# Block sums of values from the chunks already loaded, instead of a second load

## The chip, the cores and the metric

The kernel runs on one core of a Trainium2 chip. The time is the device time of one execution in microseconds; all times below are microseconds unless marked ns. A core has five engines that run side by side and wait for each other through semaphores: TensorE (PE: matmuls, with its weight loads shown as PEld), VectorE (DVE), ScalarE (ACT), GpSimd (POOL) and SyncE (SP). Transfers are issued from queues; here GpSimd issues the loads that convert float32 to bfloat16, and SyncE issues crossbar transposes (DMA_TRANSPOSE: 16-bit data turned on the way from SBUF to SBUF) and a part of the output stores. All of them are carried out by the same 16 transfer engines.

## What is computed

For 4 batches of 8 heads, 768 tokens and head dimension 64, a sparse attention followed by a gated feed-forward block:

```python
k_sum = k.reshape(B, H, nb, block, D).max(axis=3)          # block = 32, nb = 24
v_sum = v.reshape(B, H, nb, block, D).mean(axis=3)
scores_l = scale * q @ k.T          where |i - j| < 16, else -1e9
scores_s = scale * q @ k_sum.T + log(block)
a = softmax(concat(scores_l, scores_s))
x = a @ concat(v, v_sum)            # then 3072 tokens x 512
g, val = x @ w_gate, x @ w_val      # 512 -> 1536
out = x + sigmoid(x @ w_res) * ((gelu(g) * val) @ w_out)
```

So each query looks at its 31 nearest keys and at 24 block summaries: the maximum of the keys of a block and the mean of its values. The change concerns the mean of the values.

## The kernel before

**Units.** The work goes in 8 units of 384 tokens, two for each batch; unit u computes the feed-forward block of half u % 2 of batch u // 2, and in its second part the attention of unit u + 1. A unit has 12 steps `fo`: `fo_step` runs four matmuls for g (w_gate) and four for vv (w_val, L398), ScalarE makes the gelu `ge` (L404), VectorE multiplies it with vv to `gvT` (L405). After the steps follow, interleaved, the scores of the next unit (`s_step`, L330), their exponent (L336, L339) and mask (L347), the attention output (`av_step`, L362, with the normalization L370 and L372 that gives `xn`), the gate matmuls (`res_step`, L416), the output matmuls `f` (`ffn_step`, L432) and `end_step` (L437, L439, and the store of 256 KB, L443). The attention output must be turned into `xT` before the next unit's first matmuls. For units 0 to 2 this is done wholly by TensorE (`xt_step`, transposes `xp` in L381, copied by ScalarE); from unit 3 on three of the four head pairs are turned by crossbar on SyncE's queue (`xt_dma`, L386) and one by TensorE. From unit 3 on a unit opens with twelve matmuls `gv` (L544) in which the third head pair is used last.

**Data of a batch.** Keys and queries come as rows `k_sb`, `q_sb` (`load_rows`, L175, 16 loads of 96 KB from GpSimd's queue). For batches 2 and 3 they are turned by crossbar, three transposes a head pair (`turn_batch`, L251 and L254), into the window layout `kW` and into `qT`; `k_rest` then makes on VectorE the block maxima and the neighbor columns, five operations a head pair (L209 to L215). Values come as chunks of 128 tokens straight into the window layout `vext` (`load_values`, L100, seven loads), where each even window tile is a whole chunk of 128 consecutive tokens, shifted by 16. `v_spread` (L291, L294) copies them into the odd tiles, and `vsum_bc` (L300, L303) writes the block means into rows 96 to 127 of every tile.

**Block means of values.** Batch 0 and 1 get them by matmuls (`vsum_sum`). For batches 2 and 3 the values are loaded a second time as rows `v_sb` (eight more loads in `load_rows`), turned by crossbar (`turn_values`, four transposes, L261), summed by VectorE in four reductions (`block_sums`, L267, at the last four steps of units 2 and 4), turned back (`turn_sums`, L271, in units 3 and 5) and spread with the factor 1/32.

**Order.** The order on every engine is that of the program text; each engine works through its own list and waits where data are missing. A copy on GpSimd of one element of `gvT` (`gate`, L169) holds back the loads behind it until a given step is done. PSUM and SBUF buffers are taken from pools in turn; the pool `mm` of four PSUM banks holds g, vv, gv, r and f.

The places that matter below: batch 2 is loaded in unit 1, behind the gate at step 6, keys, queries and second values first, chunks last; batch 3 is loaded from the end of unit 2 (gate at step 11) and its chunks at the beginning of unit 3. In units 2 and 4 SyncE turns `v_sb` and the first two head pairs at step 0; in units 3 and 5 it turns the sums and the other two head pairs at step 0, and `k_rest` runs at steps 0, 2, 9 and 10. In unit 1 `k_rest` of head pairs 2 and 3 of batch 1 runs at steps 8 and 9.

Of the kernel before, what the change touches and what calls it, by code (L numbers as in the profile page):

```python
# [9 lines left out]
BF16 = mybir.dt.bfloat16  # L10
# [5 lines left out]
def kernel(  # L16
# [11 lines left out]
    nc = tc.nc  # L28
# [43 lines left out]
    warm = const.tile([128, 512], BF16, name="warm")  # L72
    kW = [[const.tile([128, NT, 128], BF16, name=f"kW{i}_{p}") for p in range(NP)] for i in range(2)]
    qT = [[const.tile([128, S], BF16, name=f"qT{i}_{p}") for p in range(NP)] for i in range(2)]
    vext = [const.tile([128, NT, H, D + 1], BF16, name=f"vext{i}") for i in range(2)]
    vsum = [const.tile([128, H, D + 1], BF16, name=f"vsum{i}") for i in range(2)]
    tick = const.tile([1, 1], BF16, name="tick")
    vsT = const.tile([128, NP, 128], BF16, name="vsT")
    vsB = const.tile([128, NP, 128], BF16, name="vsB")
    w_gate = wpool.tile([128, KO, DFF], BF16, name="w_gate")  # L80
    w_val = wpool.tile([128, KO, DFF], BF16, name="w_val")
    w_out = wpool.tile([128, FO, DM], BF16, name="w_out")
# [16 lines left out]
        dst = vext[b % 2][0 if c else WIN:128, 2 * c, :, 0:D] if c < NC else vext[b % 2][64:64 + WIN, NT - 1, :, 0:D]  # L99
        nc.gpsimd.dma_start(out=dst, in_=v[b, :, lo:hi, :].rearrange("h p d -> p h d"))  # L100

    k_sb, q_sb, v_sb, vT = {}, {}, {}, {}

    with tc.manual_schedule():

        def vext_consts(i):
            nc.vector.memset(vext[i][:, :, :, D:D + 1], 1.0)
            nc.vector.memset(vext[i][0:WIN, 0], 0.0)
            nc.vector.memset(vext[i][64:96, NT - 1], 0.0)
            nc.vector.memset(vext[i][64:64 + WIN, NT - 1, :, D:D + 1], 1.0)  # L110
# [58 lines left out]
            nc.gpsimd.tensor_copy(tick[:], t)  # L169

        def load_rows(b):
            for sb, src, name in ((k_sb, k, "k_sb"), (q_sb, q, "q_sb"), (v_sb, v, "v_sb"))[0:2 if b == 1 else 3]:
                sb[b] = (qk1 if sb is v_sb else qk).tile([128, NP, NC, 2 * D], BF16, tag=name, name=name)
                for h in range(H) if b > 1 else (4, 5, 6, 7, 0, 1, 2, 3):
                    nc.gpsimd.dma_start(out=sb[b][:, h // 2, :, h % 2 * D:h % 2 * D + D],  # L175
                                        in_=src[b, h].rearrange("(c p) d -> p c d", c=NC))

        def load_batch(b):
            load_rows(b)
            for c in range(NC + 1):  # L180
                load_values(b, c)

        def turn_pair(src, hp, pool, tag):

# [71 lines left out]
                    in_=q_sb[b][:, hp].rearrange("p c d -> p (c d)"))  # L256

        def turn_values(b):
            vT = qk1.tile([128, NP, S], BF16, tag="k0", name="vT")
            for hp in range(NP):  # L260
                nc.sync.dma_start_transpose(out=vT[:, hp].rearrange("d (c m) -> d c m", c=NC),  # L261
                                            in_=v_sb[b][:, hp].rearrange("p c d -> p (c d)"))
            return vT

        def block_sums(vT, hp):
            with nc.allow_low_precision("block means are bf16 operands"):
                nc.vector.tensor_reduce(out=vsT[:, hp, 96:96 + NB], in_=vT[:, hp].rearrange("d (n w) -> d n w", w=BLK),  # L267
                                        axis=mybir.AxisListType.X, op=ALU.add)

        def turn_sums():  # L270
# [25 lines left out]
        def vsum_bc(b, hp, lo, hi):  # L296
            dst = vext[b % 2][96:128, lo:hi, 2 * hp:2 * hp + 2, 0:D]
            if b < 2:
                src = vsum[b][96:128, 2 * hp:2 * hp + 2, 0:D]
                nc.vector.tensor_copy(dst, src.unsqueeze(1).to_broadcast([32, hi - lo, 2, D]))  # L300
            else:
                src = vsB[96:128, hp].rearrange("p (h d) -> p h d", d=D)
                nc.vector.tensor_scalar_mul(dst, src.unsqueeze(1).to_broadcast([32, hi - lo, 2, D]), 1.0 / BLK)  # L303

        def s_tiles(two=None):
# [145 lines left out]
        def values_step(u, fo):  # L451

            b = u // 2 + 1
            if u in (2, 4) and fo >= FO - NP:
                block_sums(vT[b], fo - FO + NP)
            if u in (3, 5):
                if fo in (1, 3):
                    v_spread(b, 0, HT // 2, fo // 2)
                if 5 <= fo < 9:
                    vsum_bc(b, fo - 5, 0, HT)  # L460
            if u % 2 == 0 and u < NU - 1:
                if fo in (0, 1):
                    v_spread(b - 1, HT // 2, NC, fo)
                if 2 <= fo < 2 + NP:
                    vsum_bc(b - 1, fo - 2, HT, NT)
# [47 lines left out]
            av_part(0, hp, st, *homes[hp], blocks=False)  # L513
        keep_warm(1, wp)
        vsum_sum(0, *MM, (5,), vs, first=False, last=True)
        vsum_out(0, vs, 0, 2, nc.vector.tensor_copy)
        vsum_out(0, vs, 2, 8, nc.scalar.copy)
        for hp in range(NP):
# [3 lines left out]
        firsts = [(w_gate, 0, two[:, 0, :]), (w_val, 0, two[:, 1, :]), (w_gate, 1, None), (w_val, 1, None)]  # L522
        for hp in range(NP):
            xt_step(0, hp, st, *(MM, MM, AO, TT)[hp], nc.scalar.copy)
            if hp:
                firsts = [(w, fo, half_fo(st, w, fo, hp - 1, hp, acc)) for w, fo, acc in firsts]

        for u in range(NU):
# [2 lines left out]
            n = u + 1  # L531
            if u == 1:
                turn_batch(1, 2, NP)
            if u == 3:
                for c in range(NC + 1):
                    load_values(3, c)
            gvT = upool.tile([128, FO, TU], BF16, tag="gvT", name="gvT")
            if u > 2:
                firsts = [(w, fo, ps_mm.tile([128, 512], F32, tag="mm", name="gv"))
# [6 lines left out]
            for fo in range(FO):  # L546
                if u == 0 and fo < 2:
                    for w, _, acc in firsts[2 * fo:2 * fo + 2]:
                        half_fo(st, w, fo, KO - 1, KO, acc)
                    fo_end(gvT, fo, firsts[2 * fo][2], firsts[2 * fo + 1][2])  # L550
                elif u > 2 and fo == 0:
                    fo_end(gvT, fo, firsts[0][2], firsts[1][2])
                elif u > 2 and fo == 1:
                    fo_end(gvT, fo, firsts[2][2], half_fo(st, w_val, fo, 0, KO))
                else:
                    fo_step(st, gvT, fo)
                values_step(u, fo)
                if u == 0 and fo == 4:
                    nc.vector.memset(vsT[:], 0.0)
                    load_rows(1)  # L560
                if u == 0 and fo == 6:
                    vext_consts(1)
                if u == 0 and fo == FO - 1:
                    kw_consts(1)
                    for c in range(NC + 1):
                        load_values(1, c)
                if u == 2 and fo == FO - 1:
                    gate(gvT[0:1, fo, 0:1])
                    load_rows(3)
                if half == 0 and 1 < nb < B and fo == 0:  # L570
                    vT[nb] = turn_values(nb)
                    turn_batch(nb, 0, NP - 2)
                if half == 1 and 1 < nb < B and fo == 0:
                    turn_sums()
                    turn_batch(nb, NP - 2, NP)
                if half == 1 and 1 < nb < B and fo in (0, 2, 9, 10):
                    k_rest(kW[nb % 2][(0, 2, 9, 10).index(fo)])
                if u == 1 and fo == 6:
                    gate(gvT[0:1, fo, 0:1])
                    load_batch(2)  # L580
                if u == 1 and fo in (1, 2, 6, 7):
                    home = TT if fo % 2 else AO
                    if fo < 4:
                        k_step(nb, fo - 1, *home)
                    else:
                        q_step(q_sb[nb], nb, 0, S, fo - 6, *home)
                if u == 1 and fo in (8, 9):
                    k_rest(kW[1][fo - 6])
                if u == 0 and fo >= FO - 4:
                    k_later(kW[0][fo - FO + 4])  # L590
                if u == 0 and fo in (FO - 3, FO - 2):
                    for hp in range(2 * (fo - FO + 3), 2 * (fo - FO + 3) + 2):
                        q_step(qb, 0, TU, S, hp, *(TT if hp % 2 else AO))
# [57 lines left out]
            s_step(n, 3, nst, two=(MM, MM), masked=False)  # L651
            if u < 2:
                mask_part(3, nst)
                xt_step(n, 0, nst, *AO, nc.scalar.copy)
                ffn_step(st, gvT, 1, 6, FO)
                xt_step(n, 1, nst, *TT, nc.scalar.copy)
                res_step(st, 2)
                av_step(n, 2, nst, *AO)
                av_step(n, 3, nst, *TT)
                end_step(u, st, 1)  # L660
                ffn_step(st, gvT, 2, 0, 7)
                xt_step(n, 2, nst, *AO, nc.scalar.copy)
                ffn_step(st, gvT, 2, 7, 10)
            else:
                xt_dma(0, nst)
                xt_dma(1, nst)
                mask_part(3, nst)
                end_step(u, st, 0)
                ffn_step(st, gvT, 1, 0, FO)
                av_step(n, 2, nst, *AO)  # L670
                xt_dma(2, nst)
                av_step(n, 3, nst, *TT)
                res_step(st, 2)
                end_step(u, st, 1)
                ffn_step(st, gvT, 2, 0, 10)
# [34 lines left out]
```

## Time and profile before

| | |
|---|---|
| median of 5 runs | 262.83 (262.47 to 264.88) |
| the profiled execution's own time | 263.37 |
| its span | 261.5 |
| TensorE busy | 251.0 (96%), 2235 matmuls |
| VectorE busy | 177.6 (68%) |
| ScalarE busy | 128.1 (49%) |
| GpSimd busy | 101.2 (39%), nearly all of it issuing loads in the first half |
| transfers issued by GpSimd (queue 0) | 86640 packets, 19.11 MB |
| transfers issued by SyncE (queue 1) | 32480 packets, 10.99 MB |
| read from HBM | 32.51 MB |

Durations are those of one profiled execution, counted from the span's start. The busy time of TensorE is modelled, since matmuls overlap. "Idle before" in brackets is the time an engine stood still before an instruction, with what ended it. A transfer has two times: how long its issue held the queue, and how long it took from issue to landing. The clock row (PEclk) gives the share of TensorE's full clock that was granted in each of 40 slices of the span, in tenths.

### The profile page before, as it was taken

What the parts mean: (1) busy time and instruction counts of PE and PEld (TensorE: products, weight loads), DVE (VectorE), ACT (ScalarE), POOL (GpSimd) and SP (SyncE); (2) the same over time, 40 slices, a digit from 0 to 9 for tenths busy, and PEclk for the clock granted to TensorE, in tenths of its full rate; (3) what the DMA queues carried; (4) which work ended last, traced back from release to release, by engine and by line L of the source; (5) the groups of instructions that cost most, each with busy time, mean ns of one, the idle gap of its engine ahead of it and who ended that gap; (6) DMA issues with size and microseconds to landing.
All of it is one profiled execution on the core that took longest, in us unless ns stands there. A gap on an engine that the chain in (4) does not pass through costs nothing.

```text
span 261.5 us, 5722 instructions
## 1 busy us (share of the span) xinstructions
PE 251.0 (96%) x2235; PEld 139.9 (53%) x2235; DVE 177.6 (68%) x426; ACT 128.1 (49%) x220; POOL 101.2 (39%) x139
## 2 busy tenths in 40 slices
PE   7989999999998999968999999999999999999994
PEld 3545655566544555534555565456545565556544
DVE  4655866594697878757786787588868764674424
ACT  3665369455635637332364435734364536443310
POOL 7996452994789901997370200010000100020000
PEclk9999999999999999997999999999999999999999
DMA  8999999999999999999999695047102200030012
GB/s 154 150 154 196 196 205 195 150 210 129 139 150 157 174 120 148 118 178 203 144 152 80 169 122 90 3 118 160 31 1 74 94 3 0 18 126 27 1 40 80
DMA packets 119146, 30.45 MB, mean 116 GB/s; under 512 B 106064, under 2 KB 116752, under 8 KB 119120
## 3 DMA queue, kind: packets, MB, share of 16 engines
q0 software_dynamic: 86640, 19.11, 85.5%
q1 hardware_dynamic: 32480, 10.99, 25.8%
q8 instruction: 17, 0.28, 0.5%
q14 instruction: 9, 0.07, 0.1%
HBM read 32.51 MB, written 6.29 MB: 148 GB/s over the span
## 4 chain that ended last, share of the span: by engine, by line
PE 83%; DMA 7%; DVE 4%; ACT 2%; POOL 1%; issue 1%; DVEq 0%
PE vv L398 21%; PE g L398 20%; PE f L432 20%; PE r L416 7%; PE gv L544 3%; PE ao L362 3%; DMA k_sb<-in_k_dram 3%; DMA xT<-xn 3%; PE s L330 3%; DMA kf<-in_k_dram 1%; PE xp L381 1%; POOL k_sb L175 1%; DVE th L437 1%; DVE xn L372 1%; DVE o L439 1%; PE tp L226 1%
## 5 line engine op out<-in xcount | busy, mean ns | idle before, releaser
L398 PE MATMUL vv<-xT,w_val 128*128 128x384 bf16 x360 | 74.6, 329 | 0.0
L404 ACT ACTIVATE ge<-g 128x384 f32<-128x384 f32 x85 | 41.8, 491 | 63.6 <-PE g L398 34.9
L398 PE MATMUL g<-xT,w_gate 128*128 128x384 bf16 x340 | 70.5, 329 | 0.0
L432 PE MATMUL f<-w_out,gvT 128*128 128x512 bf16 (+2 forms) x312 | 67.8, 363 | 0.0
L405 DVE TENSOR_TENSOR gvT<-ge,vv 128x384 bf16<-128x384 f32 x90 | 49.1, 550 | 24.6 <-PE vv L398 23.1
L398 PEld LDWEIGHTS <-w_val 128*128 128x128 bf16 x364 | 35.8, 98 | 23.9 <-issue 0.7
L398 PEld LDWEIGHTS <-w_gate 128*128 128x128 bf16 x344 | 33.7, 99 | 22.3 <-issue 1.0
L432 PEld LDWEIGHTS <-gvT 128*128 128x128 bf16 x312 | 28.5, 98 | 29.1
L443 POOL DMA_DIRECT2D out_dram<-o x12 | 6.5, 544 | 91.8 <-DVE rz L370 76.9
L422 ACT ACTIVATE th<-r 128x512 f32<-128x512 f32 x24 | 14.2, 602 | 26.9 <-PE r L416 26.9
L437 DVE SCALAR_TENSOR_TENSOR th<-th,f 128x512 f32<-128x512 f32 (+2 forms) x26 | 16.7, 642 | 12.5 <-PE f L432 8.5
L416 PE MATMUL r<-w_res,xT 128*128 128x512 bf16 x96 | 24.4, 380 | 0.0
L100 POOL DMA_DIRECT2D vext<-in_v_dram x28 | 23.2, 872 | 2.9 <-PE vv L398 1.4
L175 POOL DMA_DIRECT2D k_sb<-in_k_dram x24 | 19.7, 842 | 11.8 <-DMA w_out<-in_moe_w_out_dram 5.2
L347 DVE TENSOR_TENSOR P<-P,maskt 128x768 bf16<-128x768 bf16 x28 | 15.3, 556 | 8.1 <-ACT P L336 4.2
L175 POOL DMA_DIRECT2D q_sb<-in_q_dram x24 | 20.0, 860 | 1.3 <-DMA k_sb<-in_k_dram 0.7
L372 DVE TENSOR_TENSOR xn<-ao,rz 128x384 bf16<-128x384 f32 x32 | 17.8, 558 | 1.1
L439 DVE SCALAR_TENSOR_TENSOR o<-th,xn 128x512 f32<-128x512 f32 (+2 forms) x26 | 16.9, 651 | 0.9
L336 ACT ACTIVATE P<-s,bias_t 128x384 bf16<-128x384 f32 x32 | 16.8, 579 | 1.1 <-PE s L330 1.1
L339 ACT ACTIVATE P<-s,bias_t 128x768 bf16<-128x768 f32 x16 | 14.5, 904 | 4.3 <-PE s L330 4.3
L383 ACT COPY xT<-xp 128x384 bf16<-128x384 bf16 x17 | 8.0, 482 | 15.8 <-PE xp L381 14.1
L175 POOL DMA_DIRECT2D v_sb<-in_v_dram x16 | 13.2, 853 | 4.1 <-DMA q_sb<-in_q_dram 3.7
(99 smaller groups left out, 238.5 us busy)
## 6 DMA issues: line engine op xcount, KB each, us to landing
out_dram<-o POOLq DMA_DIRECT2D x12, 256.0 KB, 2.4
out_dram<-o SPq DMA_DIRECT2D x11, 256.0 KB, 5.7
vext<-in_v_dram POOLq DMA_DIRECT2D x20, 128.0 KB, 6.8
k_sb<-in_k_dram POOLq DMA_DIRECT2D x24, 96.0 KB, 7.3
q_sb<-in_q_dram POOLq DMA_DIRECT2D x24, 96.0 KB, 5.8
w_gate<-in_moe_w_gate_dram POOLq DMA_DIRECT2D x6, 256.0 KB, 8.4
w_val<-in_moe_w_val_dram POOLq DMA_DIRECT2D x6, 256.0 KB, 8.9
w_out<-in_moe_w_out_dram POOLq DMA_DIRECT2D x3, 512.0 KB, 15.1
```

The costliest lines, as they stand in the source:

```text
L100: nc.gpsimd.dma_start(out=dst, in_=v[b, :, lo:hi, :].rearrange("h p d -> p h d"))
L175: nc.gpsimd.dma_start(out=sb[b][:, h // 2, :, h % 2 * D:h % 2 * D + D], in_=src[b, h].rearrange("(c p) d -> p c d", c=NC))
L336: nc.scalar.activation(P[:, hh].rearrange("p t q -> p (t q)"), s[hh][:, 0:TU], AF.Exp, scale=scale, bias=bias_t[:])
L347: nc.vector.tensor_mul(Pf, Pf, maskt.unsqueeze(1).to_broadcast([128, 2 * HT, QT]))
L372: nc.vector.tensor_mul(xn, ao[:, :, :, 0:D], rz.to_broadcast([128, NSUB, 2, D]))
L398: nc.tensor.matmul(acc[:, 0:TU], w[:, ko, fs], st["xT"][:, ko, :], start=(ko == 0), stop=(ko == KO - 1))
L404: nc.scalar.activation(ge[:], g[:, 0:TU], AF.Gelu)
L405: nc.vector.tensor_mul(gvT[:, fo, :], ge[:], vv[:, 0:TU])
L416: nc.tensor.matmul(r[:], st["xT"][:, ko, ss], w_res[:, ko, :], start=(ko == 0), stop=(ko == KO - 1))
L432: nc.tensor.matmul(st["f", sub][:, 0:c1 - c0], gvT[:, fo, ss], w_out[:, fo, c0:c1], start=(fo == 0), stop=(fo == FO - 1))
L437: nc.vector.scalar_tensor_tensor(th, th, 1.0, f[:, 0:c1 - c0], ALU.add, ALU.mult)
L439: nc.vector.scalar_tensor_tensor(o[:, 0:c1 - c0].rearrange("p (k d) -> p k d", d=128), th.rearrange("p (k d) -> p k d", d=128), 0.5, st["x ...
```

## The change

The block sums of batches 2 and 3 are made from the value chunks in `vext`, and the second load of values, `v_sb`, goes away. `turn_values` now turns the seven chunks (six of 128 rows, one of 16) of 640 columns each, which are the 8 x 65 columns of a chunk and a rest that is padding or lies in the next tile; there are five reductions instead of four, the last on 8 partitions, and the turn back takes five blocks instead of four. For the columns beyond a chunk some memsets are added. Around this the order changes:

- values are loaded before keys and queries (`load_batch`), for batch 2 in unit 1 behind the gate at step 6, for batch 3 in unit 3 behind a gate at step 1; nothing is loaded at the end of unit 2;
- `turn_values` is issued at the last step of units 1 and 3, a unit earlier in the program; `turn_batch` turns all four head pairs at step 0 of units 2 and 4; `turn_sums` is issued at the last step of those units;
- `block_sums` run at steps 6 to 10 of units 2 and 4;
- `k_rest` in units 3 and 5 runs at steps 0, 2, 4 and 9; in unit 1 the two sets of batch 1 run after the last step;
- in the tail of unit 1 three `f` matmuls are put ahead of the first `xt_step`; at the start of the kernel three warming matmuls on zeros are added.

```diff
-    vext = [const.tile([128, NT, H, D + 1], BF16, name=f"vext{i}") for i in range(2)]
+    VR = H * (D + 1)
+    NG = VR // 128 + 1
+    vflat = [const.tile([128, (NT - 1) * VR + NG * 128], BF16, name=f"vext{i}") for i in range(2)]
+    vext = [t[:, 0:NT * VR].rearrange("p (t h d) -> p t h d", t=NT, h=H) for t in vflat]
...
         def load_rows(b):
-            for sb, src, name in ((k_sb, k, "k_sb"), (q_sb, q, "q_sb"), (v_sb, v, "v_sb"))[0:2 if b == 1 else 3]:
-                sb[b] = (qk1 if sb is v_sb else qk).tile([128, NP, NC, 2 * D], BF16, tag=name, name=name)
+            for sb, src, name in ((k_sb, k, "k_sb"), (q_sb, q, "q_sb")):
+                sb[b] = qk.tile([128, NP, NC, 2 * D], BF16, tag=name, name=name)
...
         def load_batch(b):
-            load_rows(b)
             for c in range(NC + 1):
                 load_values(b, c)
+            load_rows(b)
...
         def turn_values(b):
-            vT = qk1.tile([128, NP, S], BF16, tag="k0", name="vT")
-            for hp in range(NP):
-                nc.sync.dma_start_transpose(out=vT[:, hp].rearrange("d (c m) -> d c m", c=NC),
-                                            in_=v_sb[b][:, hp].rearrange("p c d -> p (c d)"))
+            vT = qk1.tile([128, NG, S + WIN], BF16, tag="k0", name="vT")
+            for c in range(NC + 1):
+                rows, t, m = (slice(0, 128), 2 * c, 128) if c < NC else (slice(64, 64 + WIN), NT - 1, WIN)
+                nc.sync.dma_start_transpose(out=vT[:, :, c * 128:c * 128 + m],
+                                            in_=vflat[b % 2][rows, t * VR:t * VR + NG * 128])
             return vT
 
-        def block_sums(vT, hp):
+        def block_sums(vT, g):
+            p = min(128, VR - g * 128)
             with nc.allow_low_precision("block means are bf16 operands"):
-                nc.vector.tensor_reduce(out=vsT[:, hp, 96:96 + NB], in_=vT[:, hp].rearrange("d (n w) -> d n w", w=BLK),
+                nc.vector.tensor_reduce(out=vsT[0:p, g, 96:96 + NB],
+                                        in_=vT[0:p, g, WIN:].rearrange("d (n w) -> d n w", w=BLK),
                                         axis=mybir.AxisListType.X, op=ALU.add)
...
-            if u in (2, 4) and fo >= FO - NP:
-                block_sums(vT[b], fo - FO + NP)
+            if u in (2, 4) and 6 <= fo < 6 + NG:
+                block_sums(vT[b], fo - 6)
...
+        keep_warm(1, wp)
         vsum_out(0, vs, 0, 2, nc.vector.tensor_copy)
...
+            if hp == 0:
+                keep_warm(2, wp)
...
-            if u == 3:
-                for c in range(NC + 1):
-                    load_values(3, c)
...
-                if u == 2 and fo == FO - 1:
+                if half == 1 and b + 2 < B and fo == (6 if b == 0 else 1):
                     gate(gvT[0:1, fo, 0:1])
-                    load_rows(3)
+                    load_batch(b + 2)
+                if half == 1 and b + 2 < B and fo == FO - 1:
+                    vT[b + 2] = turn_values(b + 2)
                 if half == 0 and 1 < nb < B and fo == 0:
-                    vT[nb] = turn_values(nb)
-                    turn_batch(nb, 0, NP - 2)
-                if half == 1 and 1 < nb < B and fo == 0:
+                    turn_batch(nb, 0, NP)
+                if half == 0 and 1 < nb < B and fo == FO - 1:
                     turn_sums()
-                    turn_batch(nb, NP - 2, NP)
-                if half == 1 and 1 < nb < B and fo in (0, 2, 9, 10):
-                    k_rest(kW[nb % 2][(0, 2, 9, 10).index(fo)])
-                if u == 1 and fo == 6:
-                    gate(gvT[0:1, fo, 0:1])
-                    load_batch(2)
+                if half == 1 and 1 < nb < B and fo in (0, 2, 4, 9):
+                    k_rest(kW[nb % 2][(0, 2, 4, 9).index(fo)])
...
-                if u == 1 and fo in (8, 9):
-                    k_rest(kW[1][fo - 6])
+                if u == 1 and fo == FO - 1:
+                    k_rest(kW[1][2])
+                    k_rest(kW[1][3])
...
             if u < 2:
                 mask_part(3, nst)
+                ffn_step(st, gvT, 1, 6, 9)
                 xt_step(n, 0, nst, *AO, nc.scalar.copy)
-                ffn_step(st, gvT, 1, 6, FO)
+                ffn_step(st, gvT, 1, 9, FO)
                 xt_step(n, 1, nst, *TT, nc.scalar.copy)
```

## The prediction

> **What bounds the kernel now.** I read the page's chain and clock row first, then the stretch table cut at unit starts, then the timelines of TensorE, SyncE, GpSimd and VectorE around the one stretch that stands out.
>
> ```profile
> PEclk9999999999999999997999999999999999999999
> ...
> PE vv L398 21%; PE g L398 20%; PE f L432 20%; PE r L416 7%; PE gv L544 3%; PE ao L362 3%; DMA k_sb<-in_k_dram 3%; DMA xT<-xn 3%; PE s L330 3%; DMA kf<-in_k_dram 1%; PE xp L381 1%; POOL k_sb L175 1%; DVE th L437 1%; DVE xn L372 1%; DVE o L439 1%; PE tp L226 1%
> ```
>
> The end is set by matmuls; what is not matmul in the chain and can go is the transfer xT<-xn, and the only dent in the clock lies in slice 19 (about 118 to 124 us). The stretch table, one row per unit, beginning with unit 1 (columns: stretch, its length, then busy time by engine, granted clock, share of the transfer engines):
>
> ```profile
> 52.15:85.23 33.08, 32.17 (x284) 18.35 (x283) 24.57 (x58) 17.49 (x31) 26.86 (x34) 1.00 2.13 157
> 85.23:113.60 28.37, 28.37 (x244) 15.74 (x243) 21.96 (x40) 14.32 (x25) 15.62 (x21) 1.00 1.83 142
> 113.60:146.93 33.33, 30.37 (x245) 16.25 (x244) 23.92 (x56) 14.20 (x25) 16.79 (x22) 0.95 1.79 147
> 146.93:175.29 28.36, 28.36 (x245) 15.73 (x243) 21.23 (x40) 14.20 (x25) 1.62 (x4) 1.00 0.54 95
> ```
>
> Units 2, 4, 5 and 6 are TensorE without a gap, 28.36 each: no change can shorten them, it can only make them longer. Unit 3 is 33.33, so 4.97 lie there. Its TensorE timeline shows where:
>
> ```profile
> 114.92 0.48 PE L544 MATMUL gv<-xT,w_gate 128*128 128x384 bf16 x2 [0.99 <-DMA xT<-xn]
> ...
> 118.35 0.32 PE L544 MATMUL gv<-xT,w_gate 128*128 128x384 bf16 x1 [1.97 <-DMA xT<-xn]
> ...
> 119.68 1.48 PE L398 MATMUL g<-xT,w_gate 128*128 128x384 bf16 x4
> ```
>
> Two waits, 2.96 together; then the group that takes 0.81 elsewhere takes 1.48: from vv at 118.83 to the first scores at 134.25 are 15.42, in unit 4 (148.88 to 162.62) 13.74, so 1.68 go to the halved clock. What the waits wait for:
>
> ```profile
> 105.31 1.25 SPq L254 DMA_TRANSPOSE qT<-q_sb  x1
> 107.16 2.56 SPq L386 DMA_TRANSPOSE xT<-xn  x2
> 110.49 0.33 SPq L443 DMA_DIRECT2D out_dram<-o  x1
> 111.19 1.23 SPq L386 DMA_TRANSPOSE xT<-xn  x1
> ```
>
> ```profile
> 103.85 6.58 POOL L175 DMA_DIRECT2D k_sb<-in_k_dram  x8 [0.52 <-issue]
> 110.35 2.53 POOL L175 DMA_DIRECT2D q_sb<-in_q_dram  x3
> ```
>
> The first answer below is of these three xT transposes, the second of the three that open unit 4:
>
> ```profile
> DMA to landing us min/median/max: 6.4/6.4/7.1
> ```
>
> ```profile
> DMA to landing us min/median/max: 2.3/2.4/2.4
> ```
>
> So unit 3 starts late because its xT transposes share the transfer engines with the k and q loads of batch 3, released at 103.15, and with crossbar work issued just before them.
>
> **The change, part by part.**
>
> *Loads of batch 3 leave unit 2 (gain 4.97).* The gate goes from the last step of unit 2 to step 1 of unit 3, so nothing of L175 is issued from 103.85 to about 118. The xT transposes then meet a quiet machine, as in unit 4. Worth 2.96 of waits, 0.33 of slowed gv groups around them and 1.68 of clock: 4.97. What is late next there: SyncE. Before xT it now has 12 turns of batch 2 and the turn of the sums, 13 instead of the 10 that ran from 88.51 to 106.56. They can start behind the output of unit 1 at 86.94 and take about 1.3 each unloaded, to 104; xn is ready near 106.5. Under load, issues took 2.5 (vT, 9.87 for 4), so xT may leave up to 1.5 late. The third xT has 4.0 from issue to use and a store of 256 KB in front of it. I take +0.2; bounds 0 and +1.5.
>
> *The same loads fall into unit 3 (+1.0).* 23 loads (7 of values, 16 of rows) begin near 118 and take 0.82 to 0.87 each, 19.5 without waits; the 31 of before took 32.3 (103.85 to 136.19), 1.04 each, so 24 at that rate: issue ends at 138 to 142, landing 6 to 7 later. The xT of unit 4, issued at 140.48, 141.89 and 144.51 before and some 4.8 earlier now, meet them. Their slack: the third landed at 146.9 and is used at 148.39 (the gv group of 147.90, after three matmuls of 0.16), so 1.5, the second has 2.9, the first 4.0. Nearest row: an SP store alone in its queue, issued at 76.82 amid GpSimd loads, landed after 4.7; the next, at 85.04, after 5.7; GpSimd's stores in the quiet units land in 2.4. Delays of 2.3 and 3.3 against 1.5 of slack give 0.8 and 1.8. I take +1.0, without a clock drop (the wait of 0.84 at 79.19 had none). Bounds: 0, if the loads end early, and +4.97, if the picture of unit 3 repeats.
>
> The Trainium skill, "DMA: Bandwidth & Descriptors", section "Queues, rings and completion order", says each transfer engine goes round its queues packet by packet, so a short transpose would not stand behind the loads of another queue; by that the term would be 0. The trace speaks against taking it whole: xT issued at 111.19 landed after 7.1 with only two transposes and a store of its own queue ahead.
>
> *Values turned from the chunks; no second load.* Per batch it removes 8 loads (0.85 of GpSimd each) and 4 turns, and adds 7 turns of 5 blocks on SyncE: about 9 of issue instead of 5. For batch 2 they stand from about 71 (first values issued at 63.3, landing 7 to 8 later) to 82, ahead of the stores of unit 1 alone, whose buffers have a unit of time; for batch 3 at 123 to 133, ahead of the xT of unit 4 near 136. Cost 0; if loads stretch them (2.5 each), they end near 138 and cost what the last paragraph bounds. Five block sums instead of four at 0.95, at steps 6 to 10: one with its gvT is 1.33 (97.20 to 98.53) against a step of 1.30, so 0.15 of lag, hidden by the spare PSUM buffers.
>
> *Neighbor keys of batches 2 and 3 earlier (+1.0).* In units 3 and 5 the sets of five VectorE operations of k_rest go from steps 0, 2, 9, 10 to 0, 2, 4, 9. Unit 5 before:
>
> ```profile
> 178.11 0.35 DVE L209 TENSOR_TENSOR km<-kW 128x384 bf16<-128x384 bf16 x1
> ...
> 179.33 0.54 DVE L405 TENSOR_TENSOR gvT<-ge,vv 128x384 bf16<-128x384 f32 x1
> ...
> 183.62 1.02 DVE L405 TENSOR_TENSOR gvT<-ge,vv 128x384 bf16<-128x384 f32 x2
> ```
>
> A set is 1.22. Put between the two gvT of 183.62, it moves the end of step 5's from 184.64 to 185.86. The g matmuls of step 8 take the PSUM buffer that this operation frees, and start at 185.69: 0.2 lost. In unit 3 a set took 1.36 (119.76 to 121.12) and copies behind it 0.63 and 0.73 instead of 0.36, while GpSimd issued loads; with that the walk gives 0.6 to 1.2. I take 0.8 and 0.2; bounds 0 and 2.
>
> *Neighbor keys of batch 1 later; three f matmuls ahead of xp in unit 1.* VectorE waited 0.55 and 1.85 for kW between 66 and 70.2; now the last three gvT pass first and the two sets (1.23 each) run from 69.7 to 72.2: the masks start at 72.2 instead of 72.39. Nothing, unless kW lands after 70.9. The three f matmuls (0.65) fill the wait of 0.84 before xp at 79.19: −0.65, bounds 0 and −0.85.
>
> *Three warm matmuls at the start*, 0.22 each, into waits of 0.39 (before ao, 19.35) and 0.35 (before xp, 21.30): +0.1, bounds 0 and +0.3; the clock was full there, so no gain. Memsets of 0.1 to 0.3 run while VectorE is idle: 0.
>
> Sum: −4.97 + 0.2 + 1.0 + 1.0 − 0.65 + 0.1 = −3.3. The profiled execution took 263.37 (span 261.5), so 260.05; it lies 0.54 over the median of five, 262.83, which gives **259.5**.
>
> **Rivals.**
>
> *The stall only moves* (263.4): the xT of unit 4 land in 6.4 to 7.1 as those of unit 3 did, so 4.97 come back in place of my 1.0. For it: loads are still landing when they are issued. Against: no turn of k or q is queued right before them, and stores go by GpSimd from unit 3 on. Chance 0.22.
>
> *SyncE late in unit 2* (261.5): the 13 issues run at 1.6 or more each, xT leaves 1.5 to 2 later, and half of the waits stay. Chance 0.12.
>
> *Slower* (266 and up): behind 23 loads and 7 stretched turns the third xT of unit 4 takes as long as the second value loads did in the window from 100 to 147, 11.1 at the median. Wait 11.1 − 2.4 − 1.5 = 7.2, clock 1.7: 8.9 instead of 1.0, 267.4. It decides from a latency of about 6.6 (a tie: 4.2 given back), and is slower by 1% from about 9.2. Chance 0.16.
>
> **How the numbers follow.** Forecast 0.50. A measurement of this kernel can tell about 1% (2.6) from no change. Faster by more: the forecast up to 260.2, and little of the second rival, 0.52; slower by more: the third rival's far part and a VectorE term at its bound, 0.14; the rest, 0.34. The range goes from 257.2 (all unknowns at their lower ends) to 264.8 (the moved stall with the upper VectorE bound), which leaves out most of the slower rival.
>
> **What would show it.** Unit 3's first gv group without a wait and a full clock in slice 19; xT of unit 3 landing in 2.3 to 3.3. For the cost: the wait of gv on xT at the start of unit 4, 0 to 2, and GpSimd loads still landing there; gaps before g at step 8 of units 3 and 5, 0.2 to 1. Wait of xp in unit 1 at 0.2. The forecast is wrong if unit 4's start shows more than 3, or a dent in the clock.

## The result, and the profile after

The kernel before took 262.94 (median of 79 executions, 260.69 to 266.01), the changed one 264.39 (44 executions, 261.87 to 268.0). The ratio is 1.0038, 95% interval 1.0021 to 1.0055: a loss of 1.0, clear of zero but under the 1% that the prediction asks of a difference, where 3.3 of gain were forecast. The ratio leaves out slow executions, those over 1.5% above the fastest of their kernel, so it says less than the medians, which lie 1.45 apart. The profiled execution of the changed kernel took 266.93 (span 265.2), 2.5 over its median, so the sizes below are those of a long execution; the traces of the experiments are set beside it.

The page of the changed kernel, first the clock row, then the two queues (packets, MB, busy share). The clock is still halved once, but in slice 23 (146 to 152) in place of 19. GpSimd's queue lost 12544 packets and 1.57 MB, as the removed loads should give.

```profile
PEclk9999999999999999999999799999999999999999
...
q0 software_dynamic: 74096, 17.54, 75.0%
q1 hardware_dynamic: 34496, 11.49, 27.3%
```

The stretch table of the changed kernel, units 1 to 5 (columns as before: stretch, its length, busy time by engine, granted clock, transfer share, GB/s):

```profile
52.05:86.25 34.20, 32.38 (x285) 18.26 (x284) 24.64 (x58) 17.42 (x31) 22.57 (x29) 1.00 2.14 141
86.25:114.77 28.52, 28.52 (x244) 15.73 (x243) 21.92 (x41) 14.46 (x25) 4.15 (x6) 1.00 1.29 144
114.77:147.49 32.72, 29.02 (x244) 15.69 (x243) 24.26 (x58) 15.16 (x26) 20.77 (x26) 1.00 1.51 129
147.49:178.56 31.07, 30.21 (x244) 16.32 (x244) 21.07 (x40) 13.16 (x24) 1.31 (x4) 0.95 0.79 116
178.56:207.21 28.65, 28.53 (x244) 15.72 (x243) 22.65 (x56) 14.18 (x25) 1.62 (x4) 1.00 0.12 39
```

Against 33.08, 28.37, 33.33, 28.36 and 28.36 that is +1.12, +0.15, −0.61, +2.71 and +0.29: together 3.66 of the 3.7 between the two spans. A stretch begins with the first matmul of its unit, so a wait before that matmul (0.99 at unit 4) counts in the stretch before it. The old stall is not gone from unit 3, there is a new one at unit 4, and unit 1 has grown. The chain of the changed kernel (start, length, what) passes through each of these places:

```profile
62.80 9.78 DMA kW<-k_sb
...
78.19 1.79 DVE vext L308 x4
...
116.05 2.61 DMA xT<-xn
...
124.96 0.69 DVE vext L302
128.36 0.81 PE g L407 x4
...
141.33 7.31 DMA xT<-xn
148.68 3.29 PE gv L553 x11
```

TensorE's timeline at the same places (start, length, line, operation, in brackets the idle time before it and what ended it):

```profile
78.61 0.38 PE L371 MATMUL ao<-vext,P 128*64 128x65 bf16 x12 [1.54 <-DVE vext L308]
...
116.06 0.48 PE L553 MATMUL gv<-xT,w_gate 128*128 128x384 bf16 x2 [0.96 <-DMA xT<-xn]
...
118.70 0.32 PE L553 MATMUL gv<-xT,w_gate 128*128 128x384 bf16 x1 [1.18 <-DMA xT<-xn]
...
128.36 0.81 PE L407 MATMUL g<-xT,w_gate 128*128 128x384 bf16 x4 [0.57 <-DVE gvT L414]
...
147.49 0.32 PE L553 MATMUL gv<-xT,w_gate 128*128 128x384 bf16 x1 [0.99 <-DMA xT<-xn]
148.68 0.49 PE L553 MATMUL gv<-xT,w_gate 128*128 128x384 bf16 x2 [0.86 <-DMA xT<-xn]
149.00 1.04 PE L553 MATMUL gv<-xT,w_val 128*128 128x384 bf16 x3
```

The 0.57 before g in unit 3 is the price of the earlier neighbor keys on VectorE (r2 below is without it). Units 3 and 4 both wait for xT, for different reasons. First the landing of the three xT of unit 3, then of unit 4:

```profile
DMA to landing us min/median/max: 2.3/2.3/2.6
...
DMA to landing us min/median/max: 6.6/7.3/7.5
```

At unit 3 the transfer is as quick as in a quiet machine; it is issued late. SyncE's timeline of the changed kernel (start, length, line, transfer):

```profile
89.06 3.15 SPq L255 DMA_TRANSPOSE kW<-k_sb  x2
96.75 1.21 SPq L258 DMA_TRANSPOSE qT<-q_sb  x1
...
112.39 2.49 SPq L395 DMA_TRANSPOSE xT<-xn  x2
...
126.05 11.90 SPq L267 DMA_TRANSPOSE vT<-vext  x7
139.91 5.20 SPq L395 DMA_TRANSPOSE xT<-xn  x3
```

Its xn was ready at 108.03 and xT left at 112.39. Ahead of it the queue stood from 92.2 to 96.75 at the first query turn, whose rows come last now that values are loaded first: they landed from 94.0 to 101.6, in the kernel before from 78.2 to 82.7. At unit 4 the xT leave with their xn, but seven value turns stand in front of them in the same queue (the last landed at 145) and loads land until 152.9.

In unit 1 VectorE stood before the last set of neighbor keys:

```profile
72.68 0.36 DVE L213 TENSOR_TENSOR km<-kW 128x384 bf16<-128x384 bf16 x1 [1.64 <-DMA kW<-k_sb]
```

The last kW landed at 72.58 (before: 70.1), and the masks, the spreading of values and the means (L308), for which `ao` waits at 78.61, followed.

### The profile page after: what moved, and what is told of

It is laid out like the page before. It is cut to its first block, busy times and chain, and to the rows that moved or that the text cites. A ratio compares the mean times of both kernels' runs of the same rounds, so it can differ in the third digit from the quotient of the medians.

```text
span 265.2 us, 5755 instructions
## 1 busy us (share of the span) xinstructions
PE 251.4 (95%) x2238; PEld 139.2 (52%) x2238; DVE 177.8 (67%) x432; ACT 127.9 (48%) x220; POOL 88.6 (33%) x123
## 4 chain that ended last, share of the span: by engine, by line
PE 59%; DMA 20%; POOL 9%; DVE 7%; issue 2%; ACT 1%; SPq 0%; DVEq 0%; POOLq 0%
PE f L441 16%; PE vv L407 15%; PE g L407 14%; PE r L425 6%; DMA w_out<-in_moe_w_out_dram 6%; DMA w_gate<-in_moe_w_gate_dram 4%; DMA xT<-xn 4%; DMA kW<-k_sb 4%; PE gv L553 4%; DMA vext<-in_v_dram 3%; POOL q_sb L179 2%; POOL vext L103 2%; PE ao L371 2%; PE s L339 2%; POOL w_gate L164 1%
## 5 line engine op out<-in xcount | busy, mean ns | idle before, releaser
L407 PE MATMUL g<-xT,w_gate 128*128 128x384 bf16 x340 | 69.7, 326 | 0.7 <-DVE gvT L414 0.6
L179 POOL DMA_DIRECT2D k_sb<-in_k_dram x24 | 20.5, 858 | 13.0 <-DMA w_out<-in_moe_w_out_dram 5.2
L553 PE MATMUL gv<-xT,w_gate 128*128 128x384 bf16 x40 | 10.3, 351 | 4.0 <-DMA xT<-xn 4.0
```

The source lines that it names most:

```text
L407: nc.tensor.matmul(acc[:, 0:TU], w[:, ko, fs], st["xT"][:, ko, :], start=(ko == 0), stop=(ko == KO - 1))
L553: nc.tensor.matmul(acc[:, 0:TU], w[:, ko, fo * 128:(fo + 1) * 128], st["xT"][:, ko, :], start=(ko == 0), stop=(ko == 2), skip_group_check= ...
```

## Experiments

The kernel before ran in each group on the same chip; ratios are to it, with their 95% intervals.

### The changed kernel again

> The changed kernel once more, for a second profile, since its first profiled execution (266.93) lies 2.5 above its median. All theories: the same three losses in smaller or larger size: gv of unit 3 waits about 2 for xT that left SyncE 4 late, gv of unit 4 waits about 2 for xT that took 7 to land, and VectorE of unit 1 waits for kW before the second set of k_rest. If one of the three is missing here, it was a matter of that one execution. Time 263 to 265.5.

262.93 (10 executions) against 262.04; ratio 1.0019 (0.9978 to 1.006). This profiled execution has a span of 260.2: unit 1 took 32.37, unit 3 waited 0.29, and the clock was full, while unit 4 waited 2.59 (1.59, 0.74 and 0.26). So the loss at unit 4 is there in a short execution too; those at unit 1 and unit 3 vary. The halved clock also comes and goes, in both kernels: in the executions of this study 38 of 81 of the kernel before had a mean granted clock under 0.996 and took 263.4 on average, the others 262.2; of the changed kernel it was 23 of 54, with 265.2 against 263.2.

### Unit 3: SyncE's list

r5 turns the last two head pairs of batches 2 and 3 in units 3 and 5, with `k_rest` at its old steps, as the kernel before does, which takes six turns out of SyncE's list ahead of unit 3's xT:

```diff
                 if half == 0 and 1 < nb < B and fo == 0:
-                    turn_batch(nb, 0, NP)
+                    turn_batch(nb, 0, NP - 2)
+                if half == 1 and 1 < nb < B and fo == 0:
+                    turn_batch(nb, NP - 2, NP)
...
-                if half == 1 and 1 < nb < B and fo in (0, 2, 4, 9):
-                    k_rest(kW[nb % 2][(0, 2, 4, 9).index(fo)])
+                if half == 1 and 1 < nb < B and fo in (0, 2, 9, 10):
+                    k_rest(kW[nb % 2][(0, 2, 9, 10).index(fo)])
```

> The changed kernel with the turns of head pairs 2 and 3 of batches 2 and 3 back in units 3 and 5 (and k_rest at 0, 2, 9, 10, which this needs). Theory SyncE: in unit 2 only six turns and that of the sums stand ahead of xT, it leaves at about 107.5 instead of 112.4, the waits of gv in unit 3 (2.14) go; unit 4 gets six more turns into its loads, so its wait stays at 1.9 or grows to 3: 1 to 3 faster than the changed kernel, 261.5 to 263.5. Rival: SyncE waits for the q rows of batch 2 in any case and xT stays 2 or more late: at most 1 faster.

266.07 (4 executions, all with a halved clock), ratio 1.0151 (1.0095 to 1.0206): slower than the kernel before, where a gain of 1 to 3 over the changed kernel was expected. The trace of r5, TensorE at the start of unit 3 and of unit 4:

```profile
113.03 0.65 PE L553 MATMUL gv<-xT,w_gate 128*128 128x384 bf16 x3
...
145.76 0.32 PE L553 MATMUL gv<-xT,w_gate 128*128 128x384 bf16 x1 [4.20 <-DMA xT<-xn]
147.02 0.80 PE L553 MATMUL gv<-xT,w_gate 128*128 128x384 bf16 x2 [0.94 <-DMA xT<-xn]
```

Unit 3 opens without a wait (xT issued at 106.60, with its xn, landing after 2.3): SyncE's list was the cause there. But the six turns now stand in unit 3 among the loads, the value turns behind them ran until 138.2, and unit 4 waits 5.1 where it waited 1.85.

r9 leaves all turns where the change has them and only turns the keys of all pairs ahead of the queries:

```diff
             for hp in range(p0, p1):
                 kt = kW[b % 2][hp].rearrange("d (c e) m -> d c e m", e=2)
                 for e in range(2):
                     nc.sync.dma_start_transpose(
...
+            for hp in range(p0, p1):
                 nc.sync.dma_start_transpose(
                     out=qT[b % 2][hp].rearrange("d (c m) -> d c m", c=NC),
```

> The changed kernel with one edit: for each batch SyncE issues the turns of the keys of all its pairs first and those of the queries after them (before: keys, keys, queries pair by pair). Theory (SyncE's order): in unit 2 of the changed kernel the first query turn stood until its rows had landed (issued 96.75), everything behind it moved, the three xT were issued 4.4 us after their xn and unit 3 waited 2.14 us; in unit 1 the last key pair landed at 72.58 and VectorE, waiting for it, cost TensorE 1.7. With the keys first, eight turns fill the time until the queries are there, the xT of unit 3 are issued with their xn (no wait at unit 3), and the last key pair of unit 1 lands 1.3 to 3 us earlier (unit 1 about 32.0 long instead of 32.0 to 34.2). Unit 4 stays as it is (xT landing after 6.6 to 8, some 2.5 of waits). Ratio to the kernel before 0.994 to 1.000. Rival (the 16 DMA engines are full and the order is of no matter): the xT of unit 3 are still 2 to 4 us late, ratio 1.002 to 1.005.

262.06 (12 executions) against 263.21, ratio 0.9953 (0.9922 to 0.9984), within what the theory gave. SyncE's timeline of r9:

```profile
88.29 12.01 SPq L255 DMA_TRANSPOSE kW<-k_sb  x8
100.47 6.35 SPq L259 DMA_TRANSPOSE qT<-q_sb  x4
106.92 1.22 SPq L280 DMA_TRANSPOSE vsB<-vsT  x1
108.30 2.49 SPq L396 DMA_TRANSPOSE xT<-xn  x2
```

The list doesn't stand before the queries. The first xT is still 1.8 behind its xn, the third 1.3, which the slack that the prediction read at unit 4 (4.0 and 1.5) covers, and unit 3 has no wait. Unit 1 took 32.75, with 0.39 of wait before `ao`. Unit 4 kept waits of 2.7, the largest loss that is left.

### Unit 4: loads, turns, or both

r4 leaves out the 23 loads of batch 3, r7 the seven turns of its values; r6 is the kernel before with all of batch 3 loaded behind step 1 of unit 3, its second load of values included.

```diff
 r4
-                    load_batch(b + 2)
+                    if b == 0:
+                        load_batch(b + 2)
+                    else:
+                        k_sb[3], q_sb[3] = k_sb[2], q_sb[2]
 r7
-                    vT[b + 2] = turn_values(b + 2)
+                    vT[b + 2] = turn_values(b + 2) if b == 0 else vT[2]
 r6
-            if u == 3:
-                for c in range(NC + 1):
-                    load_values(3, c)
...
-                if u == 2 and fo == FO - 1:
+                if u == 3 and fo == 1:
                     gate(gvT[0:1, fo, 0:1])
-                    load_rows(3)
+                    load_batch(3)
```

> The changed kernel without any load of batch 3 (its keys, queries and values are those left in the buffers; the seven turns of values and all other work stay). Theory loads: xT of unit 4 lands in 2.4 instead of 7, the two waits of gv (1.85) and the halved clock (1.7) go, also part of the slowed VectorE copies: 3.5 to 4 faster than the changed kernel (260.5). Rival crossbar: the seven turns of values ahead of xT on SyncE are what delays it; the loads matter little: latency stays above 5, at most 1 faster (263.5). The wait at unit 3, which theory SyncE puts down to batch 2, stays at 2 under both.

> The changed kernel without the seven turns of the values of batch 3 (its block sums are made from those of batch 2; all loads stay). Theory loads: xT of unit 4 still takes 6 to 7, the loads end some 3 to 4 earlier, a part of the wait goes: 1 to 2 faster (263). Rival crossbar: latency of xT falls to 3, waits and clock (3.5) go: 260.8.

> The kernel before with one part of the change alone: batch 3 (rows, second values, chunks) is loaded behind step 1 of unit 3. Theory: xT of unit 3 lands in 2.4, waits and clock of 4.97 go there; 31 loads instead of 23 then run through the tail of unit 3 and into unit 4, so xT of unit 4 lands in 7 to 10 and 5 to 8 come back: 263 to 266. If the move itself were a gain and the rest of the change spoils it: 258 to 260.

r4: 259.78, ratio 0.9904 (0.9871 to 0.9936). r7: 260.1, 0.9922 (0.9887 to 0.9957). r6: 262.35, 0.9982 (0.9948 to 1.0016). The landing of the three xT of unit 4, for r4, r7 and r6:

```profile
DMA to landing us min/median/max: 2.3/2.3/2.5
```

```profile
DMA to landing us min/median/max: 2.8/4.7/4.9
```

```profile
DMA to landing us min/median/max: 5.7/6.3/6.4
```

The first xT is issued some 6.4 ahead of the unit and the others have a shorter lead. In r4 and r7 unit 4 doesn't wait. In r6 the first landing is just hidden and the other two are not:

```profile
145.11 0.48 PE L541 MATMUL gv<-xT,w_gate 128*128 128x384 bf16 x2 [1.07 <-DMA xT<-xn]
...
147.04 0.32 PE L541 MATMUL gv<-xT,w_gate 128*128 128x384 bf16 x1 [0.47 <-DMA xT<-xn]
```

Leaving out either the 23 loads or the seven turns takes the wait away: r4 came out as the theory of the loads said, r7 as its rival, the crossbar, said. My reading is that the turns keep xT's own queue full, that the loads slow every transfer, and that the turns stretch the loads too (in r7 the last query load landed at 144.1, in the changed kernel at 152.9). Two limits: in r4 the turns, with no chunks to wait for, were issued by 125.1 and xT at 136.15, so turns that stand right ahead of xT without loads were not run; and r6, with SyncE's queue empty ahead of xT, shows that loads alone are enough when they are 31 in place of 23.

r6 also shows no gain from the gate alone: unit 3 lost its stall, unit 4 got 1.87 of one, unit 3 began 1.7 later than in the first trace of the kernel before, and the time stayed.

### Neighbor keys

r2 puts `k_rest` of units 3 and 5 back to steps 0, 2, 9 and 10 (the second half of r5's diff); r3 puts that of unit 1 back to steps 8 and 9:

```diff
-                if u == 1 and fo == FO - 1:
-                    k_rest(kW[1][2])
-                    k_rest(kW[1][3])
+                if u == 1 and fo in (8, 9):
+                    k_rest(kW[1][fo - 6])
```

> The changed kernel with k_rest of units 3 and 5 back at steps 0, 2, 9, 10. Theory VectorE: the waits of g on gvT at step 8 (0.57 in unit 3, some 0.3 in unit 5) go, 0.9 faster than the changed kernel (263.5). Rival transfers: unit 3 then reaches its end earlier while the same loads are still landing, the wait of gv in unit 4 grows by as much, and only the 0.3 of unit 5 stays: 264.1.

> The changed kernel with the two sets of k_rest of unit 1 back at steps 8 and 9. Theory order: the first set runs under the steps again, the masks of unit 1 come up to 1.2 earlier, and the wait of ao of 1.74 falls to about 0.5: 1 faster than the changed kernel (263.4). Rival transfers: the masks wait for the landing of the last kW transposes in either place (72.58 in the profile), the second set ends at the same time and nothing changes: 264.4.

r2: 263.46, ratio 1.0057 (1.0021 to 1.0093). r3: 264.17, 1.0045 (1.0002 to 1.0088). Neither is faster than the changed kernel. In r2's trace the wait of 0.57 in unit 3 and the 0.29 of unit 5 are gone (28.36), as the VectorE term says, but 0.9 doesn't show in the median: 6 of its 10 executions had a halved clock against 2 of 10 of r1, and why is open. In r3 unit 1 took 32.74; with the later place it took 34.20, 32.37, 33.71, 32.14, 31.95 and 31.95 in the six traces that have it and the change's order of turns, 32.7 on average. So with one and the same place the unit varies by 2.25 between traces, and was longest where kW landed latest (72.58). No gain of either place shows, though there is only this one trace of the changed kernel with the earlier place.

### Spreading the work of batch 3

r8 undoes the moved turns and neighbor keys, and moves part of batch 3 into unit 4: the queries' loads behind step 1, the value turns to step 0. r10 is r9 with the value turns of batch 3 at step 0 of unit 4 and their sums a step later, the last two head pairs of batch 3 turned in unit 5, and `k_rest` at 0, 2, 9 and 10. r11 is r10 with the queries of batch 3 loaded behind step 3 of unit 4, and the first turns of batch 3 at that step. Core of r10, and of what r11 adds:

```diff
-                if half == 1 and b + 2 < B and fo == FO - 1:
-                    vT[b + 2] = turn_values(b + 2)
-                if half == 0 and 1 < nb < B and fo == 0:
-                    turn_batch(nb, 0, NP)
+                if u in (1, 4) and fo == (FO - 1 if u == 1 else 0):
+                    vT[u // 2 + u % 2 + 1] = turn_values(u // 2 + u % 2 + 1)
+                if half == 0 and 1 < nb < B and fo == 0:
+                    turn_batch(nb, 0, NP if u == 2 else NP - 2)
...
+                if u == 5 and fo == 0:
+                    turn_sums()
+                    turn_batch(nb, NP - 2, NP)
...
+                if u == 4 and fo == 3:
+                    gate(gvT[0:1, fo, 0:1])
+                    load_rows(3, (1,))
```

> A version made from both: block sums from the chunks; turns of head pairs 2 and 3 and of the sums in units 3 and 5 as before; of batch 3 only values and keys are loaded in unit 3, the queries behind step 1 of unit 4, and its values are turned in unit 4; k_rest at the places of before. If both theories hold (SyncE for unit 3, loads for unit 4), neither unit waits for xT and the clock stays full: 4 to 5 under the kernel before, 258 to 259.5. If only one holds: 260.5 to 262.

> As r9, and the seven turns of the value chunks of batch 3 are issued at the start of unit 4, behind the xT (they stood at the end of unit 3's first stage, ahead of them), their sums at steps 7 to 11; the last two pairs of batch 3 are turned in unit 5, and the neighbor keys in units 3 and 5 stand at steps 0, 2, 9 and 10. All loads of batch 3 stay in unit 3. Theory (turns and loads together make the xT of unit 4 late, either alone is hidden): xT landing after 3 to 5 us, which the 6.4 us ahead of unit 4 hide; no wait at unit 4 and no halved clock there; ratio to the kernel before 0.984 to 0.990. Rival (the loads alone are enough): the xT still land after 6 to 8 us, 1.5 to 2.5 us of waits at unit 4, ratio 0.993 to 0.998. Rival (the stall only moves on): the turns, 1.3 us each on SyncE, make the sums or the xT of unit 5 late, 1 us or more at units 4 and 5, ratio 0.993 to 0.997.

> As r10, and the eight loads of the queries of batch 3 wait for step 3 of unit 4, so that unit 3 has 15 of the 23 loads. If loads still delay the xT of unit 4 in r10, this is 0.5 to 2 us faster than r10 (ratio to the kernel before 0.980 to 0.987). If r10's xT are already hidden, the two are alike within 0.3%. If the loads now meet the value turns in unit 4 (the sums late, VectorE waiting at step 7), this is slower than r10 by 0.5 to 1.5 us.

r8: 260.32, ratio 0.9921 (0.9893 to 0.995). r10: 258.01, 0.9796 (0.9747 to 0.9845). r11: 257.57, **0.9772** (0.9727 to 0.9816), 2.3% faster than the kernel before and the best here. r8 took 0.8 more than the 259.5 at most that was expected if neither unit waits for xT: neither did, but it had waits of 0.95 and 0.78 on VectorE, behind a key turn among the loads and behind the value turns. r10 is under the 0.984 to 0.990 of its theory. The xT of its unit 4 landed so:

```profile
DMA to landing us min/median/max: 3.4/5.0/5.1
```

That is hidden, and there is no wait at unit 4: with the turns away, the loads may stay in unit 3, and r11 differs by 0.2%, as expected for that case. The stretch table of r11, units 1 to 4:

```profile
51.75:83.70 31.95, 31.69 (x282) 18.19 (x284) 23.88 (x58) 17.40 (x31) 22.52 (x29) 1.00 2.03 149
83.70:112.06 28.36, 28.20 (x241) 15.74 (x243) 22.27 (x41) 14.30 (x25) 4.43 (x6) 1.00 1.36 160
112.06:140.43 28.37, 28.21 (x242) 15.76 (x243) 23.28 (x56) 14.20 (x25) 13.41 (x18) 1.00 1.06 99
140.43:168.79 28.36, 28.20 (x241) 15.75 (x243) 22.34 (x41) 14.20 (x25) 8.58 (x13) 1.00 1.08 131
```

Every unit from 2 on is at the 28.36 that TensorE needs.

r12 asks what the second load itself costs: the kernel before with both loads of values, keys first, the loads of batch 3 spread over units 3 and 4, and its first turns at step 3 of unit 4, as in r11.

```diff
-                if u == 2 and fo == FO - 1:
+                if u == 3 and fo == 1:
                     gate(gvT[0:1, fo, 0:1])
-                    load_rows(3)
+                    load_rows(3, (2, 0))
+                if u == 4 and fo == 1:
+                    gate(gvT[0:1, fo, 0:1])
+                    load_rows(3, (1,))
+                    for c in range(NC + 1):
+                        load_values(3, c)
```

> The kernel before with its second load of the values kept, and its loads of batch 3 placed as r11 has them: unit 3 loads values and keys behind step 1 (16 loads), unit 4 the queries and then the value chunks behind step 1 (15 loads), no load in the last step of unit 2; the keys of each batch's pairs are turned ahead of their queries. It asks whether the second load that the change removes costs anything by itself. Theory (it costs only where it meets xT): units 2 to 6 take 28.4 each, no wait at units 3 and 4; unit 1 keeps its 0.84 for xp; time some 1 us over r11: ratio to the kernel before 0.981 to 0.987. Rival (the eight loads more keep the queues full into the xT of unit 4 or 5): waits of 1 us or more at one of them, ratio 0.988 to 0.996.

258.81 against 262.7, ratio 0.9871 (0.9833 to 0.9909), at the upper end of the theory; units 3 and 4 have no wait for xT. So more than half of the 2.3% of r11 comes from where transfers stand. The rest of the change is worth 1.0% by the two ratios, which are of two chips, and 0.5% by the two medians. Of the 1.0 between the two spans (256.2 and 255.2) 0.40 is unit 1 and 0.20 unit 2; some 0.6 comes after the start of unit 7, which the change doesn't touch, and −0.18 before unit 1, so that share isn't explained.

## Why the prediction was wrong

The stall at unit 3 was rightly found, but its price came back at two places: SyncE's list in unit 2 (forecast 0.2, in the first trace 2.14) and the start of unit 4 (forecast 1.0, there 3.7). Term by term:

- **Loads leave unit 2 (−4.97): the mechanism held, the size is that of one execution.** xT of unit 3 landed after 2.3 to 2.6 (forecast 2.3 to 3.3), and where SyncE was in time (r5) unit 3 began without a wait. But 1.68 of the 4.97 was a halved clock that only about half of the executions of the kernel before have. Taking 0.54 off for the median of five didn't mend that: r12, the kernel before without a wait for xT at units 3 and 4, took 3.9 off the median, and a part of that is unit 1, 0.73 shorter in its trace.
- **SyncE late in unit 2 (+0.2, bounds 0 and +1.5): the step that failed first.** "12 turns of batch 2 and the turn of the sums ... can start behind the output of unit 1 ... to 104": the count was right, but a turn also waits for its rows, and the same edit that put the values first put the queries last. xT left 4.4 late and cost 2.14, over the upper bound; in the other traces with the same list it cost from nearly 0 (r2) to 2.3 (r7). The rival "SyncE late" had the right place with the wrong cause: not every issue was slow, the list stood once, for 4.5. r9, which changes only the order of the list, took the wait away.
- **The loads fall into unit 3 (+1.0, bounds 0 and +4.97): mis-sized.** Waits of 1.85 and 1.85 of slowed matmuls, 3.7 together (2.9 to 4.1 in r1, r2, r3 and r9). The delay was read from a store that stood alone in its queue amid loads (2.3 and 3.3 over quiet). The xT had seven turns ahead in their own queue: they were costed at 0 in the next paragraph, though they start only when the chunks land (126.05, not 123) and the last lands at 145, after xT's issue at 139.91. r7, without them, gives 2.8 to 4.9: the store was a fair row for the 23 loads, and the turns ought to have been added. The rival "the stall only moves", with the transposes of unit 3 as its row, was right at unit 4: it named 6.4 to 7.1, and they landed after 6.6 to 7.5.
- **Unit 1 (−0.65): the condition was named, its chance wasn't counted.** xp's wait is gone; but "nothing, unless kW lands after 70.9" met 72.58, and the unit grew by 1.12. In r1 it shrank by 0.71, as forecast; the mean over six traces is −0.4.
- **Neighbor keys (+1.0): right**, 0.57 in unit 3 and 0.29 in unit 5 by the trace, though the total of r2 doesn't confirm it. **Warm matmuls (+0.1)**: unit 1 begins at 52.05 against 52.15, nothing.
- **The slower rival** (third xT of unit 4 landing after 11.1) did not come: 6.6.

The ends of the range don't follow from its terms to the digit: they add up to 257.0 and 264.5, against 257.2 and 264.8. Nothing above hangs on it.

The Trainium skill says that each transfer engine takes its queues in turn, packet by packet ("DMA: Bandwidth & Descriptors", section "Queues, rings and completion order"). The prediction read from it that the loads' share would be 0, which is more than the sentence says: taking turns is sharing. With SyncE's queue empty ahead of them the xT landed after 2.3 to 2.5 without loads (r4), after 2.8 to 4.9 amid 23 (r7) and after 5.7 to 6.4 amid 31 (r6). The trace that the prediction set against it was less clean than it says: beside two transposes and a store, the turn issued at 105.31 was still in flight until 111.74.

## What to carry to other kernels

When loads are reordered, follow each reader of the one that is now last: a queue that works through its list in order, as SyncE's did here, carries that wait to everything behind it, here to the one transfer on the path. Cost a transfer by what is in flight in its own queue as well as by what other queues move, and compare the sum with its lead. Before summing a stall from a profile, ask of several executions how often it is there.

## What the runs showed of the hardware

The granted clock changed in steps of one length. Every halved stretch inside the kernels lasted 3.41, and all changes lie multiples of 3.41 apart, as the Trainium skill has it ("TensorE: Matmul & The Clock Gate", section "Part 1: The HAM clock gate": a free-running window of 3413 ns). The page speaks of an idle window; here a window in which TensorE was 42% busy was enough. The kernel before, windows on that grid (columns: window, length, TensorE busy, granted clock, transfer share, GB/s):

```profile
112.44:115.85 3.41, 2.42 (x16) 1.00 2.03 200
115.85:119.26 3.41, 1.44 (x10) 1.00 1.96 203
119.26:122.68 3.42, 3.42 (x13) 0.50 1.67 199
```

The first window holds the wait of 0.99, the second that of 1.97, with 1.44 of 3.41 busy, and the next is halved. In the traces from unit 1 on, windows with a busy share of 0.35 or less had a halved one behind them, those with 0.52 and more didn't. Between, two did (0.42 here, 0.46 in the changed kernel at 145.70) and three didn't (0.43 in r5, 0.46 in the changed kernel at 114.98, 0.47 in r9). In unit 0 of r8 even one of 0.57 did, so no sharp bound shows. r1 waited 2.59 at unit 4, more than the 1.85 of the first trace, and kept its clock, since the grid cut its waits in two windows. So whether a stall of 2 to 3 costs 1.7 more depends, at least in part, on where it falls in the grid, which stands differently to the span's start in each trace. Executions with and without a halved clock lay 1.2 and 2.0 apart on average for the two kernels, a part of why executions of one kernel differ.
